# Second head's decay rows in place, clamps on ScalarE, and later loads for heads nine and ten

## Chip, cores and metric

The kernel runs on one core of a Trainium2 chip. The metric is the device time of one execution in microseconds (us). Three runs of the kernel before took 766.26, 769.34 and 770.9 us, so the median is 769.34 us.

## The reference

Three layers follow each other, over 4 batches of 576 positions. B and H below are 4 and 8, so there are 32 attention heads of 64 columns.

```
# attention with a decay
cum    = cumsum(max(s, 0))                       # s: (4, 8, 576)
scores = q k^T / 8 - (cum_i - cum_j), causal     # per head, 576 x 576
attn   = softmax(scores);  x = attn v            # -> (4, 576, 512)
# gated values
gate   = sigmoid(5-tap causal convolution of x with conv_w)
x      = (gate * (x @ w_val)) @ w_out
# mixing of positions (rank 32), then a feed-forward layer of width 2048
u      = x + (x^T U V)^T
out    = u + max(u @ w_ch1, 0) @ w_ch2
```

## The kernel before

**Tiling.** Each head is one step of the loop at L752, `n` from 0 to 32. In step `n` the scores of head `n` are made in five row blocks (`score`, L474) and the probabilities of head `n-1` are transposed (`trans`, L509); after every second head the pair is multiplied with its values (`attn_v`, L533). Once a batch of 8 heads is done, its dense layers are mixed into the steps of the next batch. The feed-forward layer comes last, in TensorE matmuls alone. So the first eight heads run with little beside them but the splitting of the weights (`widen`, L358), which is spread over the steps as side work.

**The decay.** The term cum_j - cum_i enters the score matmul as extra contraction rows under the 64 rows of q and k. Head 0 has two such rows, made in place: VectorE clamps `s` at 0 (L256), scans it (L257) and writes one row under Q and one under K (`row`, L308) from the coefficients in `coef`. The other heads have four rows (KP), taken from E and F: for all 32 heads at once VectorE clamps `sp` (L260), scans it into `cum` (L261), rounds it (L262) and subtracts (L264), and ScalarE multiplies by -8 (L263, L265). Head 1 and head 2 fetch their rows by a transfer from there (L297, `direct`). The rest read them from a copy in device memory (`ef`, L341).

**Two kinds of heads.** Heads 0 to 7, 16 and 30 (`WHOLE`, L85) are loaded straight into their Q and K tiles and multiplied in full fp32. Every other head is loaded as one tile `qk` (`load_raw`, L276, two transfers), split by ScalarE into `hi` and by GpSimd into a rest that lies in Q2 (`prep_head`, L332 and L333), and spread by five transfers into Q1, K1, Q2 and K2 (`high` and `low`, L322 to L330). In the trace these transfers are named K<-hi, Q<-hi and K<-Q. Head 8 is the first such head. Its loads stand in the program at step 6 and head 9's at step 7, but nothing ties them to that step: they need only a free `qk` buffer, of which there are two.

**What sets the order.** All transfers go through SP's queue, in order. A planner lays out the instructions of each engine from a timed model, with a priority by program order and the offset that each kind of work has in `PLAN` (L23); what could run early by the model is moved early. Every engine then works strictly in that order: an instruction that waits holds up all that stands behind it on its engine. `fill` (L468) puts small matmuls without use between the transposes of the first heads, and 13 matmuls of the same sort (`WARM`) stand ahead of the first scores.

Of the kernel before, what the change touches and what calls it, by code (L numbers as in the profile page):

```python
# [11 lines left out]
F32 = mybir.dt.float32  # L12
F32R = mybir.dt.float32r
BF16 = mybir.dt.bfloat16
U32 = mybir.dt.uint32
AF = mybir.ActivationFunctionType
ALU = mybir.AluOpType
# [3 lines left out]


PLAN = {  # L23
    "pace": ("gpsimd", -500),
    "qk_hi": ("scalar", 6000),
    "qk_lo": ("gpsimd", 2000),
    "put": ("sync", 3000),
# [62 lines left out]
ORDER = "T0 T1 S0 T2 T3 S1 S2 S3 T4 S4 A0 A1"  # L90
NPD = 6
DT = {"exp": 0.51, "xh": 0.96, "xl": 0.25, "tap": 1.5, "taps": 0.9, "tanh": 1.83, "gv": 4.3, "nl": 3.6, "rows": 10.0, "prep": 1.51}
WARM = 13


@with_exitstack
def fused_kernel(ctx, tc, qT, kT, vP, s, wval, wout, convw, U, V, w1, w2, rows01, out):
    nc = tc.nc
    B, H, D, S = qT.shape
    P = 128  # L100
# [7 lines left out]
    KP = 4  # L108
# [5 lines left out]
    NH = B * H  # L114
# [20 lines left out]
    def rnd(kind, o, i, by=1.0):  # L135

        eng = Via(kind)
        if eng.name == "scalar":
            eng.mul(o, i, by)  # L139
        elif eng.name == "vector" and by == 1.0:  # L140
            eng.tensor_copy(o, i)
        else:
            eng.tensor_scalar(o, i, by, 0.0, op0=ALU.mult, op1=ALU.add)

    def rest(kind, o, i, hi, by=1.0):

        if by == 1.0:
            Via(kind).tensor_sub(o, i, hi.bitcast(F32))
        else:
            Via(kind).scalar_tensor_tensor(o, i, by, hi.bitcast(F32), op0=ALU.mult, op1=ALU.subtract)  # L150
# [5 lines left out]
    def defer(dt, f, key=None):  # L156
        order[0] += 1
        later.append((clock["now"] + dt, order[0], f, key))
# [56 lines left out]
    at = ctx.enter_context(tc.tile_pool(name="at", bufs=2, side="right"))  # L215
# [15 lines left out]
    def part(b, m, n=S, parts=P):  # L231
        return uT[0:parts, m, b * S:b * S + n]

    sp, cum = (part(1, m, parts=NH) for m in range(2))
    ones, first = part(1, 2), part(1, 3)
    E = [part(2, r, parts=NH) for r in range(KP)]
    F = [part(3, r, parts=NH) for r in range(KP)]
    coef = at1.tile([P, 4], F32, name="coef")
    nc.sync.dma_start(first[64:66, :], s[0, 0:1, :].to_broadcast([2, S]))
    nc.sync.dma_start(coef[64:66, :], rows01)  # L240
    nc.sync.dma_start(sp, s.rearrange("b h s -> (b h) s"))

# [2 lines left out]
    idle = psV.tile([P, 1024], F32, tag="av", name="idle")[:, 0:512]  # L245
    for _ in range(WARM):
        nc.tensor.matmul(idle, warm[:, 0:P], warm, start=True, stop=True)
# [5 lines left out]
    )  # L253
    nc.vector.memset(ones, 1.0)

    nc.vector.tensor_scalar_max(first[64:66, :], first[64:66, :], 0.0)  # L256
    nc.vector.tensor_tensor_scan(first[64:66, :], ones[64:66, :], first[64:66, :], 0.0, op0=ALU.mult, op1=ALU.add)  # L257
    for t, v in ((E[0], 8.0), (E[2], 8.0), (F[1], 1.0), (F[3], 1.0)):
        nc.gpsimd.memset(t, v)
    nc.vector.tensor_scalar_max(sp, sp, 0.0)  # L260
    nc.vector.tensor_tensor_scan(cum, ones[0:NH, :], sp, 0.0, op0=ALU.mult, op1=ALU.add)  # L261
    nc.vector.tensor_copy(F[0].bitcast(F32R), cum)  # L262
    nc.scalar.mul(E[1], F[0], -8.0)  # L263
    nc.vector.tensor_sub(F[2].bitcast(F32R), cum, F[0])  # L264
    nc.scalar.mul(E[3], F[2], -8.0)  # L265
    EF = [uT[0:NH, :, b * S:(b + 1) * S] for b in (2, 3)]


# [3 lines left out]
    hd = {}  # L272

    raw = {}

    def load_raw(n):  # L276

        if n < NH and n not in WHOLE:
            b, h = divmod(n, H)
            raw[n] = at.tile([P, S], F32, tag="qk", name="qk")  # L280
            nc.sync.dma_start(raw[n][0:64, :], qT[b, h])
            nc.sync.dma_start(raw[n][64:, :], kT[b, h])

    def load_head(n, direct=False):
        b, h = divmod(n, H)
        t = hd[n] = {"K": 64 + KP if n else 66, "nm": at.tile([P, 6], F32, tag="nm", name="nm")}
        kind = F32 if n in WHOLE else F32R
        for nm in ("Q1", "K1"):
            t[nm] = at.tile([64 + KP, S], kind, tag=nm, name=nm)
        if n in WHOLE:  # L290
            nc.sync.dma_start(t["Q1"][0:64, :], qT[b, h])
            nc.sync.dma_start(t["K1"][0:64, :], kT[b, h])
        else:
            t["qk"] = raw.pop(n)
        if n:
            for i, nm in enumerate(("Q1", "K1")):
                nc.sync.dma_start(t[nm][64:, :].bitcast(F32), EF[i][n:n + 1] if direct else ef[n, i])  # L297

    def load_values(n):
        b, h = divmod(n, H)  # L300
        hd[n]["V"] = at1.tile([P, 5, 2, D], F32, tag="V", name="V")
        nc.sync.dma_start(hd[n]["V"], vP[b, h // 2])

    def prep_head(n):

        t = hd[n]
        if n == 0:
            def row(o, i):  # L308
                nc.vector.tensor_scalar(
                    o[64:66, :], first[64:66, :], coef[64:66, 2 * i:2 * i + 1], coef[64:66, 2 * i + 1:2 * i + 2],  # L310
                    op0=ALU.mult, op1=ALU.add,
                )
            return [lambda: row(t["Q1"], 0), lambda: row(t["K1"], 1)]
        if n in WHOLE:
            return []
        t["Q2"], t["K2"] = (at.tile([P, S], F32R, tag=nm, name=nm) for nm in ("Q2", "K2"))
        hi, lo = at.tile([P, S], F32R, tag="hi", name="hi"), t["Q2"]

        def put(o, i):
            Via("put").dma_start(o.bitcast(F32), i.bitcast(F32))  # L320

        def high():  # L322
            put(t["Q1"][0:64, :], hi[0:64, :])
            put(t["K1"][0:64, :], hi[64:, :])
            put(t["K2"][0:64, :], hi[64:, :])

        def low():

            put(t["K2"][64:, :], lo[64:, :])
            put(t["Q2"][64:, :], hi[0:64, :])  # L330
        return [
            lambda: rnd("qk_hi", hi, t["qk"]),  # L332
            lambda: rest("qk_lo", lo, t["qk"], hi),  # L333
            high,
            low,
        ]

    load_head(0)
    load_head(1, True)
    for i in range(2):  # L340
        nc.sync.dma_start(ef[:, i], EF[i])  # L341

    for f in prep_head(0):
        f()
    for c in range(5):
        for x in Pt[c]:
            nc.gpsimd.memset(x[:, 0 if c == 0 else CW[c]:], 0.0)
# [33 lines left out]
    def words(ap):  # L381

        return ap.bitcast(U32)
# [40 lines left out]
    pace = []  # L424
# [5 lines left out]
    def load_wide(i):  # L430
        wait_for_pace(ring[i % 3])
        wide[i][0](ring[i % 3])
# [319 lines left out]
    for n in range(NH + 1):  # L752
        phase[0] = n
        if n > 0:
            pace[:] = [hd[n - 1]["nm"][:, 4:5]]
        if 2 <= n + 1 < NH:
            load_head(n + 1, n == 1)
        load_raw(n + 2)
        if n == 1:
            nc.sync.dma_start(craw.bitcast(U32), words(convw))  # L760
        if 1 <= n <= 3:
            load_wide(n - 1)
        if n < NH and n % 2:
            load_values(n)
        m = n - 1
        items = []

        def add(cost, f, *a):
            items.append((cost, f, a))

        ahead, before = n < NH, n > 0
        for x in (ORDER if m % 2 else ORDER0).split():
            kind, i = x[0], int(x[1])
            if kind == "S" and ahead:
                add((0.1, 0.22, 0.32, 0.42, 0.53)[i], score, n, i)
            elif kind == "T" and before:
                add((0.03, 0.21, 0.32, 0.43, 0.55)[i], trans, m, i)
            elif kind == "A" and before and m % 2:
                add((0.96, 1.7)[i], attn_v, m, i)
        if before and m % 2 == 1:  # L780
            add(0.0, norm, m // 2)
        total = sum(x[0] for x in items)
        if before and m % 2 == 1:
            defer(DT["rows"], lambda pr=m // 2: norm_rows(pr))
        if n + 1 < NH:
            for i, f in enumerate(prep_head(n + 1)):
                defer(DT["prep"] * i, f, "prep")
        todo = 0.0
        if dense:
            first, _, done, _ = dense[0]  # L790
            slots = max(1, first + H - n)
            todo = max(0.0, (DENSE - done) / slots)
        clock["dense"] = clock["att"] = 0.0
        for cost, f, a in items:
            f(*a)
            advance(cost)
            clock["att"] += cost
            if n > 0:
                steps[0] += SIDE[(n > 8) + (n > 12) + (n > 17)] * cost / total
                side_step(int(steps[0]))  # L800
                steps[0] -= int(steps[0])
            run_dense(todo * clock["att"] / total)
        if before and m % H == H - 1:
            dense.append([n + 1, dense_work(m // H), 0.0, clock["now"] + DWAIT])
        force("prep")
        if m % 2:
            hd.pop(m, None)
            hd.pop(m - 1, None)
# [192 lines left out]
```

## Time and profile before

| what | value |
|---|---|
| median of 3 runs | 769.34 us (766.26 to 770.9) |
| the profiled execution | 764.93 us, of which the trace spans 762.8 us |
| PE busy | 743.7 us (98%) |
| DVE, ACT, POOL busy | 464.4, 299.2, 291.2 us |
| chain that ended last | PE 85%, DMA 4%, DVE 4%, ACT 3% |
| mean granted TensorE clock | 0.993 |

PE is TensorE, PEld its weight loads, DVE VectorE, ACT ScalarE, POOL GpSimd, and SP (SPq: its sequencer) issues transfers. PE's busy time counts every matmul, the useless ones of the start and of `fill` too, and a matmul that runs at half clock is busy for longer; so 98% is no measure of what PE could still gain in the first microseconds. A row of a timeline or of a list of groups ends with the idle time of its engine just before and with what ended it. In the trace `uT` is also the tile in which `sp`, `cum`, `first`, E and F lie, `P` is a tile of probabilities and `nm` holds the (negated) maxima of a head's rows.

### The profile page before, as it was taken

Reading aid. Unit: us, or ns where it says so; the run is one execution under the profiler, and the core shown is the slowest. Engines: PE = TensorE matmul, PEld = TensorE weight load, DVE = VectorE, ACT = ScalarE, POOL = GpSimd, SP = SyncE. Lnnn points to the kernel's source line nnn. Section 1 sums busy time; section 2 is a strip of 40 time slices with the busy share of each in tenths; the row PEclk is TensorE's granted clock in tenths of the full one; section 3 lists DMA queues with packets and bytes.
Section 4 is the critical chain, followed back from the end, with each engine's and each line's share of the span. In section 5 each row is a group of like instructions: output and inputs, shape, how many; then the busy total and the mean of one; then the engine's idle time right before and its main releaser. Section 6 shows DMA issues by size and latency. Waiting matters only on the chain.

```text
span 762.8 us, 12349 instructions
## 1 busy us (share of the span) xinstructions
PE 743.7 (98%) x4453; PEld 624.8 (82%) x4453; DVE 464.4 (61%) x1052; ACT 299.2 (39%) x785; POOL 291.2 (38%) x321
## 2 busy tenths in 40 slices
PE   8999999899999999999899999999999999999998
PEld 4777888788887998798788888888888888888887
DVE  6798875887657755666749996424582234223234
ACT  4777756875677776633212211111121011001110
POOL 3466754553522233557197765102540024100000
PEclk9999999999999999999999999999999999999999
DMA  5734544644455432021103221100120000000023
GB/s 147 229 120 120 140 118 114 174 119 127 120 124 134 122 100 56 18 85 55 56 1 111 83 87 53 54 1 28 55 85 1 0 28 1 1 0 1 1 111 138
DMA packets 27012, 59.40 MB, mean 78 GB/s; under 512 B 4654, under 2 KB 5294, under 8 KB 26952
## 3 DMA queue, kind: packets, MB, share of 16 engines
q1 hardware_dynamic: 26952, 58.62, 26.9%
q8 instruction: 35, 0.57, 0.3%
q14 instruction: 25, 0.20, 0.1%
HBM read 37.04 MB, written 5.31 MB: 56 GB/s over the span
## 4 chain that ended last, share of the span: by engine, by line
PE 85%; DMA 4%; DVE 4%; ACT 3%; issue 2%; SPq 1%; POOL 0%; ACTq 0%; DVEq 0%
PE d L132 39%; PE acc L132 26%; PE pt L132 8%; PE av L132 6%; PE sc L132 6%; DMA qk<-in_kT 2%; DMA K<-Q 1%; DVE av L604 1%; ACT P L132 1%; DVE P L132 1%; DMA Q<-hi 1%; DVE uT L132 1%; DMA uT<-in_w 0%; ACT PTB L132 0%; ACT hi L132 0%
## 5 line engine op out<-in xcount | busy, mean ns | idle before, releaser
L132 PE MATMUL d<-u,w1h 128*128 128x512 f32 (+1 forms) x640 | 184.2, 371 | 0.0
L132 DVE SCALAR_TENSOR_TENSOR hl<-d,hh 128x512 fp32r<-128x512 f32 (+1 forms) x80 | 50.7, 635 | 170.3 <-ACT hh L861 170.3
L861 ACT ACTIVATE hh<-d 128x512 fp32r<-128x512 f32 (+1 forms) x80 | 44.2, 554 | 274.6 <-PE acc L132 149.5
L132 PEld LDWEIGHTS d<-u,w1h 128*128 128x128 f32 x640 | 116.0, 188 | 22.2
L132 PE MATMUL d<-u,w1l 128*128 128x512 f32 (+1 forms) x320 | 118.6, 371 | 0.0
L132 PE MATMUL acc<-hl,w2h 128*128 128x512 f32 (+1 forms) x320 | 105.0, 371 | 0.0
L132 PE MATMUL acc<-hh,w2h 128*128 128x512 f32 (+1 forms) x320 | 104.4, 372 | 0.5 <-DVE uT L132 0.5
L132 PE MATMUL acc<-hh,w2l 128*128 128x512 f32 (+1 forms) x320 | 102.0, 371 | 0.0
L132 ACT ACTIVATE P<-P,nm 64x64 f32<-64x64 f32 (+4 forms) x160 | 89.0, 560 | 25.2 <-DVE nm L132 24.6
L132 PE MATMUL sc<-K,Q 68*128 68x288 f32 (+11 forms) x384 | 89.1, 344 | 4.6 <-ACT PTB L132 1.8
L132 DVE CUSTOM_DVE_ANT_0 P<-sc,causal 64x64 f32<-64x64 f32 (+4 forms) x160 | 65.2, 421 | 30.8 <-PE sc L132 28.2
L132 PE MATMUL pt<-ident,P 128*128 128x128 f32 x480 | 78.5, 284 | 5.4 <-ACT PTA L139 2.6
L132 DVE TENSOR_TENSOR uT<-acc,uT 128x512 f32<-128x512 f32 (+1 forms) x120 | 70.1, 630 | 22.3 <-PE acc L132 22.2
L132 PEld LDWEIGHTS sc<-K,Q 68*128 68x128 f32 (+2 forms) x384 | 62.2, 193 | 13.2 <-ACT PTB L132 2.6
L132 PEld LDWEIGHTS d<-u,w1l 128*128 128x128 f32 x320 | 60.2, 188 | 11.0
L132 PEld LDWEIGHTS acc<-hh,w2h 128*128 128x128 f32 x320 | 58.7, 188 | 12.1 <-issue 0.9
L132 PEld LDWEIGHTS acc<-hl,w2h 128*128 128x128 f32 x320 | 58.8, 188 | 11.2
L132 PEld LDWEIGHTS acc<-hh,w2l 128*128 128x128 f32 x320 | 58.6, 188 | 11.3
L132 PEld LDWEIGHTS pt<-ident,P 128*128 128x128 f32 x480 | 56.3, 145 | 12.3 <-ACT PTA L139 3.6
L604 DVE SCALAR_TENSOR_TENSOR av<-X,cw,av 128x576 f32<-128x576 f32 x64 | 52.3, 817 | 4.9 <-ACT av L132 4.5
L132 DVE SCALAR_TENSOR_TENSOR scr<-raw,scr 128x512 uint32<-128x512 uint32 (+1 forms) x56 | 52.4, 936 | 1.4
L132 DVE TENSOR_SCALAR scr<-scr 128x512 uint32<-128x512 uint32 x56 | 43.3, 773 | 11.9 <-POOL w1l L132 6.3
(123 smaller groups left out, 1286.9 us busy)
## 6 DMA issues: line engine op xcount, KB each, us to landing
raw<-in_w SPq DMA_DIRECT2D x28, 512.0 KB
K<-hi SPq DMA_DIRECT2D x44, 144.0 KB
Q<-hi SPq DMA_DIRECT2D x44, 144.0 KB
V<-in_vP SPq DMA_DIRECT2D x16, 320.0 KB
out<-uT SPq DMA_DIRECT2D x16, 256.0 KB
qk<-in_qT SPq DMA_DIRECT2D x22, 144.0 KB
qk<-in_kT SPq DMA_DIRECT2D x22, 144.0 KB
K<-Q SPq DMA_DIRECT2D x22, 144.0 KB
```

What stands on the lines that cost most here:

```text
L132: return f(*args, **kw)
L604: Via("tap").scalar_tensor_tensor(g, X[:, k:k + S], cw[:, p, k:k + 1], g, op0=ALU.mult, op1=ALU.add,)
L861: Via("hh").activation(h_, o, AF.Relu)
```

## The change

- Head 1 gets two decay rows made in place, as head 0 has them: a second tile of `s` is loaded ahead of everything but the first, and scan and two rows are run for it on VectorE. It takes no rows from E and F any more.
- The clamps at 0 (two of the small tiles, one of `sp`) move from VectorE to ScalarE as Relu.
- The work on E and F (memsets, scan, rounding, difference, two products) comes after the rows of both heads in the program.
- The loads of heads 8 and 9 are placed in steps 3 and 4, and ahead of each GpSimd copies one column of head 2's or head 3's maxima into the tile to be loaded, so that the transfer can't be issued before that maximum is known. From head 10 on the loads stand where they stood.
- The priority offset of that copy becomes 0, and the matmuls ahead of the first scores become 10.

```diff
-    "pace": ("gpsimd", -500),
+    "pace": ("gpsimd", 0),
...
-WARM = 13
+WARM = 10
...
-    ones, first = part(1, 2), part(1, 3)
+    ones = part(1, 2)
+    first = [part(0, 0), part(0, 1)]
...
-    nc.sync.dma_start(first[64:66, :], s[0, 0:1, :].to_broadcast([2, S]))
+    for i in range(2):
+        nc.sync.dma_start(first[i][64:66, :], s[0, i:i + 1, :].to_broadcast([2, S]))
...
-    nc.vector.tensor_scalar_max(first[64:66, :], first[64:66, :], 0.0)
-    nc.vector.tensor_tensor_scan(first[64:66, :], ones[64:66, :], first[64:66, :], 0.0, op0=ALU.mult, op1=ALU.add)
-    for t, v in ((E[0], 8.0), (E[2], 8.0), (F[1], 1.0), (F[3], 1.0)):
-        nc.gpsimd.memset(t, v)
-    nc.vector.tensor_scalar_max(sp, sp, 0.0)
-    nc.vector.tensor_tensor_scan(cum, ones[0:NH, :], sp, 0.0, op0=ALU.mult, op1=ALU.add)
-    nc.vector.tensor_copy(F[0].bitcast(F32R), cum)
-    nc.scalar.mul(E[1], F[0], -8.0)
-    nc.vector.tensor_sub(F[2].bitcast(F32R), cum, F[0])
-    nc.scalar.mul(E[3], F[2], -8.0)
+    for x in first:
+        nc.scalar.activation(x[64:66, :], x[64:66, :], AF.Relu)
...
+            if H <= n < H + 2:
+                Via("pace").tensor_copy(raw[n][:, 0:1], hd[n - H + 2]["nm"][:, 4:5])
             nc.sync.dma_start(raw[n][0:64, :], qT[b, h])
...
-        t = hd[n] = {"K": 64 + KP if n else 66, ...
+        t = hd[n] = {"K": 64 + KP if n > 1 else 66, ...
...
-        if n:
+        if n > 1:
             for i, nm in enumerate(("Q1", "K1")):
                 nc.sync.dma_start(t[nm][64:, :].bitcast(F32), EF[i][n:n + 1] if direct else ef[n, i])
...
-        if n == 0:
+        if n < 2:
+            x = first[n][64:66, :]
...
-            return [lambda: row(t["Q1"], 0), lambda: row(t["K1"], 1)]
+            return [
+                lambda: nc.vector.tensor_tensor_scan(x, ones[64:66, :], x, 0.0, op0=ALU.mult, op1=ALU.add),
+                lambda: row(t["Q1"], 0), lambda: row(t["K1"], 1),
+            ]
...
-    load_head(0)
-    load_head(1, True)
+    for n in range(2):
+        load_head(n)
+    for n in range(2):
+        for f in prep_head(n):
+            f()
+    for t, v in ((E[0], 8.0), (E[2], 8.0), (F[1], 1.0), (F[3], 1.0)):
+        nc.gpsimd.memset(t, v)
+    nc.scalar.activation(sp, sp, AF.Relu)
+    nc.vector.tensor_tensor_scan(cum, ones[0:NH, :], sp, 0.0, op0=ALU.mult, op1=ALU.add)
+    nc.vector.tensor_copy(F[0].bitcast(F32R), cum)
+    nc.scalar.mul(E[1], F[0], -8.0)
+    nc.vector.tensor_sub(F[2].bitcast(F32R), cum, F[0])
+    nc.scalar.mul(E[3], F[2], -8.0)
     for i in range(2):
         nc.sync.dma_start(ef[:, i], EF[i])
-    for f in prep_head(0):
-        f()
...
-        load_raw(n + 2)
+        if 3 <= n <= 4:
+            load_raw(n + H - 3)
+        elif n + 2 >= H + 2:
+            load_raw(n + 2)
...
-        if n + 1 < NH:
+        if 2 <= n + 1 < NH:
             for i, f in enumerate(prep_head(n + 1)):
```

## Rows read from the trace of the kernel before

**Rows 1.** Busy us (instructions) of each engine by stretch, granted clock, DMA share, GB/s.

```profile
7.00:22.47 15.47, 12.83 (x70) 9.80 (x70) 7.55 (x29) 9.82 (x30) 2.03 (x2) 0.89 0.63 163
22.47:59.47 37.00, 37.00 (x273) 28.35 (x274) 32.52 (x97) 29.18 (x89) 21.83 (x24) 1.00 0.53 160
59.47:110.00 50.53, 47.62 (x371) 40.27 (x370) 41.27 (x116) 34.57 (x98) 32.40 (x34) 1.00 0.50 131
```

**Rows 2.** The chain that ended last, 6 to 23 us: start, length, what.

```profile
6.87 1.36 DVE uT L261
...
8.73 0.76 DVE uT L264
...
10.11 0.67 ACT hi L132
...
12.81 4.17 DMA K<-Q
...
17.54 0.63 SPq L297
...
22.47 0.66 PE pt L132 x4
```

**Rows 3.** Timeline of DVE, 2 to 12 us: start, length, line, operation.

```profile
2.21 1.43 DVE L256 TENSOR_SCALAR uT<-uT 2x576 f32<-2x576 f32 x1
...
5.05 0.70 DVE L260 TENSOR_SCALAR uT<-uT 32x576 f32<-32x576 f32 x1
...
6.28 0.57 DVE L309 TENSOR_SCALAR K<-uT,coef 2x576 f32<-2x576 f32 x1
...
8.25 0.45 DVE L262 CAST uT<-uT 32x576 fp32r<-32x576 f32 x1
...
9.41 0.20 DVE L132 CUSTOM_DVE_ANT_0 P<-sc,causal 64x64 f32<-64x64 f32 x1
...
11.82 0.08 DVE L132 DVE_READ_ACCUMULATOR2_ANT nm<- 128x1 f32 x1
```

**Rows 4.** Timeline of PE, 1 to 13 us.

```profile
1.52 5.03 PE L247 MATMUL idle<-causal 128*128 128x512 bf16 x13 [1.52 <-DVE causal L243]
...
6.90 3.08 PE L132 MATMUL sc<-K,Q 66*128 66x64 f32 x12 [0.34 <-DVE K L309]
...
12.47 0.60 PE L132 MATMUL sc<-K,Q 68*128 68x64 f32 x2 [0.98 <-DVE nm L132]
```

**Rows 5.** Timeline of SP's queue, 10 to 32 us.

```profile
10.37 0.61 SPq L297 DMA_DIRECT2D Q<-uT  x1
...
31.82 0.29 SPq L297 DMA_DIRECT2D K<-ef  x1
```

**Rows 6.** Busy us by stretch of one microsecond, granted clock after the five engines.

```profile
10.00:11.00 1.00, 0.19 (x2) 0.00 (x0) 1.00 (x5) 1.00 (x4) 0.14 (x1) 1.00 0.02 5
...
13.00:14.00 1.00, 1.00 (x7) 0.82 (x6) 0.23 (x2) 0.97 (x5) 0.00 (x0) 0.50 1.04 272
...
15.00:16.00 1.00, 1.00 (x6) 0.77 (x5) 0.37 (x2) 0.14 (x1) 0.00 (x0) 0.52 0.97 244
```

**Rows 7.** Timeline of ACT, 0 to 24 us.

```profile
0.73 1.28 ACT L263 ACT_TABLE_LOAD   x1 [0.73 <-PEq L991]
8.73 0.68 ACT L263 ACTIVATE uT<-uT 32x576 f32<-32x576 f32 x1 [6.72 <-DVE uT L262]
...
21.08 0.68 ACT L132 ACTIVATE hi<-qk 128x576 fp32r<-128x576 f32 x1 [1.72 <-DMA qk<-in_kT]
```

**Rows 8.** Timeline of POOL, 0 to 11 us.

```profile
0.34 0.10 POOL L991 MEMSET const-uint8-127<- 128x1 uint8 x1
...
4.09 1.02 POOL L250 TENSOR_SCALAR_AFFINE_SELECT causal<-causal 128x128 f32<-128x128 f32 x1
...
10.86 1.40 POOL L132 TENSOR_TENSOR Q<-qk,hi 128x576 fp32r<-128x576 f32 x1 [5.41 <-ACT hi L132]
```

**Rows 9.** Timeline of PE, 37 us: the first scores of head 4.

```profile
37.07 0.33 PE L132 MATMUL sc<-K,Q 68*128 68x64 f32 x2
```

More of the change, by code (lines that the diff above doesn't have):

```diff
@@ L285, in load_head @@
         b, h = divmod(n, H)
-        t = hd[n] = {"K": 64 + KP if n else 66, "nm": at.tile([P, 6], F32, tag="nm", name="nm")}
+        t = hd[n] = {"K": 64 + KP if n > 1 else 66, "nm": at.tile([P, 6], F32, tag="nm", name="nm")}
         kind = F32 if n in WHOLE else F32R
@@ L306, in prep_head @@
         t = hd[n]
-        if n == 0:
+        if n < 2:
+            x = first[n][64:66, :]
             def row(o, i):
                 nc.vector.tensor_scalar(
-                    o[64:66, :], first[64:66, :], coef[64:66, 2 * i:2 * i + 1], coef[64:66, 2 * i + 1:2 * i + 2],
+                    o[64:66, :], x, coef[64:66, 2 * i:2 * i + 1], coef[64:66, 2 * i + 1:2 * i + 2],
                     op0=ALU.mult, op1=ALU.add,
                 )
-            return [lambda: row(t["Q1"], 0), lambda: row(t["K1"], 1)]
+            return [
+                lambda: nc.vector.tensor_tensor_scan(x, ones[64:66, :], x, 0.0, op0=ALU.mult, op1=ALU.add),
+                lambda: row(t["Q1"], 0), lambda: row(t["K1"], 1),
+            ]
         if n in WHOLE:
```

## The prediction

> **What bounds the kernel now.** I read the stages first. From 22.47 to 59.47 us PE has no idle microsecond: 37.00 busy of 37.00, at full clock. From 59.47 to 110 it idles 2.9 us, and DVE still has 9.3 us to spare of 50.53 there. Before 22.47 it is another matter: of the 15.47 us from 7.00 on PE is busy for 12.83, at a mean granted clock of 0.89 [rows 1]. So the change, which touches the first heads, is worth what it takes off the time until PE runs dense, and what it puts into the dense stage counts against it.
>
> The chain of waits says what holds the start up, and it isn't PE. It runs over DVE's work on E and F (scan at 6.87, difference at 8.73), then over head 8's split on ACT (10.11), its transfer K<-Q (12.81, 4.17 us long), the issue of head 2's row that stood behind it on SP (17.54), and reaches PE again at 22.47 [rows 2]. The last stretch shows in ACT's rows: the split of head 9 at 21.08 held ACT idle for 1.72 us until its load had landed [rows 7], while an exponential that PE needs stood behind it. Work for heads 8 and 9, six steps ahead of their scores, thus lies in the chain of heads 0 to 2.
>
> Around it: head 0's scores start at 6.90, released by its K row on DVE, and take 3.08 us; head 1's start at 12.47 [rows 4]. PE is said to have waited for a maximum there, but that ended at 11.90 [rows 3]; the later event is head 1's Q row, issued at 10.37 [rows 5], so 2.1 us pass from issue to use. The first maximum comes at 9.41, because scan, rounding and difference of E and F stand ahead of it [rows 3]. From 10 to 11 us PE is busy for 0.19 us, and from 13 to 16 its granted clock is about 0.50, which is the 1.2 GHz level [rows 6].
>
> **The change, part by part.**
>
> *Head 0's rows.* The clamp leaves DVE, where it took 1.43 us from 2.21 on [rows 3], for ACT, where 576 columns take 0.68 us and the one table load ends at 2.01 [rows 7]. The clamp then ends at 2.9, the scan (1.36, as that of `cum` in rows 2) at 4.3 and the two rows (0.57 each [rows 3]) at 5.4, against 6.85 before; that also drops the `sp` clamp (0.70) that stood between them [rows 3]. Not certain: the clamp of 1.43 us lay wholly beside POOL's first memsets, the rows of 0.57 us after the last long instruction of POOL, which ends at 5.1 [rows 3, 8]. The new rows start at 4.3. If both take 1.43, they end at 7.1. So the first score moves by -1.4 to +0.3 us. I take 6.0, a gain of 0.9, since POOL's long work is over at 5.1, in the middle of the first row. One more transfer issue ahead of Q and K (at most 0.61, as the one at 10.37 [rows 5]) fits inside this, since Q and K have until 6.0.
>
> The Trainium skill (SBUF — State Buffer, the section on the two sides of SBUF) says that GpSimd and a VectorE instruction in a two-port mode lock each other out for a whole instruction. By that rule both rows could take the long time, the scores would start at 7.1, and the sum below would be 1.1 us smaller; the row of 1.43 us speaks for it, the end of POOL's work against the second row.
>
> The Trainium skill (ScalarE: Activation LUTs, Rules for kernel authors) puts relu and max on VectorE and not on ScalarE. By it the clamp should lose; the rows say 0.68 on ACT against 0.70 and 1.43 on DVE, so at most nothing is lost, and ACT is idle until 8.73 [rows 7].
>
> *Head 1's rows and the work on E and F.* DVE gains one scan and two rows (1.36 + 1.14 = 2.5 us) and loses the clamps. Head 1's scores no longer wait for E, F and a transfer. E and F are now needed by head 2 alone, whose row was issued at 17.54 [rows 2]; there is cover for them behind head 0's maxima. If that cover is gone, head 2 is late by what they take: 1.36 + 0.45 + 0.76 us on DVE, 0.68 on ACT and 2.1 for the transfer [rows 2, 3, 7].
>
> *How early can PE be dense?* Two floors, both from a first score at 6.0. DVE: 2.5 for head 1's rows, 2.6 for E and F, and twice 2.5 for the maxima of heads 0 and 1 (9.41 to 11.90 [rows 3]) end at 16.1. PE: its 12.83 busy us up to 22.47 hold three at half clock (13 to 16 [rows 6]), an estimated 11.3 us at full clock, which end at 17.3. Before, PE lay 4.1 us above its floor (15.47 - 11.3). Engines that work strictly in order don't reach such a floor: I take half of the 4.1 as gained, between nothing and all. With the start that is 0.9 + 2.1 = 3.0 us, between -0.3 and 5.5.
>
> *What is moved into the dense stage.* Heads 8 and 9 now cost it two splits on ACT (0.68 each), two rests on POOL (1.40 each), two copies on POOL (0.10 each, as its 128x1 memset) and some ten issues on SP with their transfers [rows 7, 8]. Beside 37.00 us of PE there, ACT is busy for 29.18, POOL for 21.83 and the transfer engines for 0.53 [rows 1], so most of it is hidden. Upper bound: both splits hold ACT as at 21.08, 1.72 + 0.68 us each, or 4.8 us; lower bound nothing. I take one split exposed, 0.7 us, nearer the low end since PE's rows there show no idle time at all.
>
> *The new wait.* The copy waits on POOL for the last maximum of head 2 (then 3). Behind it stand POOL's steps of the weight splitting, for which DVE waits; behind the load on SP stand loads of weights, values and the next head. Head 4's last row was issued by 32.11 [rows 5] and used at 37.07 [rows 9]; less 2.1 us for the transfer that is 2.9 us of slack, so a short wait costs nothing.
>
> *The rest.* Three warm-up matmuls fewer end it about 1.2 us earlier (13 took 5.03 [rows 4]), at 5.4, close to the new first score. The priority offset has only the two copies to act on. Neither gets a term of its own.
>
> Sum: 3.0 - 0.7 = 2.3 us gained. The profiled execution took 764.93 us (762.8 of span and 2.1 around it) and lies 4.4 us under the median of the runs; it would become 762.6, and the median of 769.34 becomes **767.0**.
>
> **Rivals.**
> 1. *The gain is absorbed* (0.22). PE's 2.9 idle us from 59.47 to 110 show waits that an earlier start lengthens if their ends hang on DVE's weight splitting. For it: DVE is busy for 32.52 of 37.00 before [rows 1]. Against: that work starts earlier too. Time: 769, within 1.5.
> 2. *POOL and SP stall* (0.12), the case on the slow side. The order is planned from a model; if the maxima come later on the chip than there, POOL stands at the copy and SP behind it. It decides from 2.9 us of stall on. A stall of 5 us at both heads costs 2 x 2.1 us, with the exposed splits 4.8; less the start's 3.0 that is +6.0, or 775. From 771 to 779. Against it: POOL idles 15 of 37 us.
> 3. *A larger gain* (0.12). Both floors are nearly reached (5.5 us) and freer queues shorten later waits, of which 2.9 us lie before 110. All of it would be 8.4 us: 761; from 757 to 763.
> 4. *The change doesn't do what it says* (0.04). The planner puts E and F ahead of head 0's maxima all the same, or gives ACT a second table load (1.28 us [rows 7]) ahead of the exponentials. Time: 768 to 771.
>
> **How the numbers follow.** The forecast has 0.50 and its own range is 763 to 769. The other cases stretch the range: 760.5 takes in most of rival 3, and 774, the bound without any gain at the start and with 4.8 us lost (769.3 + 0.3 + 4.8 = 774.4), half of rival 2. The runs before spread by 4.6 us, or 0.6%, so 1% (7.7 us) is about what a measurement can tell from no change. Faster by over 1% means under 761.6: a good half of rival 3 and some spread of the forecast, 0.13. Slower means over 777.0: a quarter of rival 2 and some mishap of a newly planned order, 0.06. The rest is 0.81.
>
> **What would show it.** In the profile after, the first score of head 0 should come near 6.0 and its first maximum before 8.5; head 1's first score before 11; no split of `qk` before 25 us; the granted clock should stay at its higher level from 13 to 16. PE should run dense from about 19.5 instead of 22.47 and show little idle time until 57. If the start comes 3 us earlier and the end doesn't, rival 1 holds. If SP shows waits of more than 2.9 us at the loads of heads 8 and 9 and PE idles between 30 and 45, rival 2 holds. Wrong altogether would be a start no earlier than before.

## The result: 1% slower

| | before | after |
|---|---|---|
| median | 769.17 us (766.26 to 770.9, 4 runs) | 775.89 us (772.69 to 780.36, 4 runs) |
| ratio, 95% interval | | 1.0101 [1.0062, 1.0141] |
| profiled execution, span | 764.93, 762.8 us | 774.55, 772.8 us |
| mean granted clock of it | 0.993 | 0.986 |

The forecast was 767.0 and its range ended at 774.0. The two profiled executions lie 9.6 us apart and the medians 6.7, since that of before was one of its shortest; so I read places in the traces, and sizes from medians.

**Stages after** (busy us and instructions of PE, PEld, DVE, ACT, POOL, then granted clock, DMA share, GB/s), to be held against [rows 1, 6]:

```profile
7.00:22.47 15.47, 15.39 (x76) 11.41 (x76) 9.14 (x41) 10.36 (x34) 0.42 (x2) 0.78 0.57 177
22.47:59.47 37.00, 34.73 (x254) 26.33 (x252) 30.88 (x88) 27.54 (x84) 22.68 (x25) 1.00 0.55 158
42.00:48.00 6.00, 4.32 (x38) 3.44 (x35) 4.84 (x12) 3.46 (x12) 2.85 (x4) 1.00 0.57 146
78.00:90.00 12.00, 9.75 (x73) 8.31 (x71) 7.07 (x23) 7.45 (x23) 8.02 (x8) 0.86 0.48 120
59.47:110.00 50.53, 45.80 (x353) 38.62 (x353) 39.21 (x110) 32.69 (x95) 30.95 (x31) 0.97 0.48 119
```

Before had from 78 to 90:

```profile
78.00:90.00 12.00, 11.68 (x92) 10.69 (x88) 10.75 (x29) 8.30 (x23) 9.86 (x9) 1.00 0.71 184
```

The stage without an idle microsecond now has 2.27 us of them, 1.68 of these between 42 and 48. From 59.47 to 110 us PE idles 4.7 us instead of 2.9, with a second hole of 2.25 us between 78 and 90, where the granted clock is 0.86 instead of 1.00. In the start PE is busier, but its granted clock is 0.78 instead of 0.89.

**The hole at 45 us.** POOL, then SP, ACT and PE of after (start, length, line, operation, and in brackets the idle time before it and what ended it):

```profile
28.21 0.19 POOL L277 COPY qk<-nm 128x1 f32<-128x1 f32 x1 [1.05 <-DVE nm L132]
...
38.76 1.28 POOL L132 TENSOR_TENSOR wvl<-uT 128x512 fp32r<-128x512 f32 x1 [0.69 <-DVE nm L132]
39.98 0.19 POOL L277 COPY qk<-nm 128x1 f32<-128x1 f32 x1
```

```profile
27.80 0.30 SPq L294 DMA_DIRECT2D K<-ef  x1
28.42 0.47 SPq L278 DMA_DIRECT2D qk<-in_qT  x1
28.94 0.59 SPq L279 DMA_DIRECT2D qk<-in_kT  x1
...
39.05 1.62 SPq L278 DMA_DIRECT2D qk<-in_qT  x2
40.71 1.88 SPq L279 DMA_DIRECT2D qk<-in_kT  x2
```

```profile
31.90 0.69 ACT L132 ACTIVATE hi<-qk 128x576 fp32r<-128x576 f32 x1 [0.31 <-DMA qk<-in_kT]
...
44.83 0.68 ACT L132 ACTIVATE hi<-qk 128x576 fp32r<-128x576 f32 x1 [2.16 <-DMA qk<-in_kT]
45.42 0.76 ACT L132 ACTIVATE P<-P,nm 128x576 f32<-128x576 f32 x1
...
46.18 0.74 ACT L132 ACTIVATE PTB<-pt 128x256 f32<-128x256 f32 x2
...
84.76 0.68 ACT L132 ACTIVATE hi<-qk 128x576 fp32r<-128x576 f32 x1 [4.45 <-DMA uT<-in_U]
```

```profile
35.87 0.43 PE L132 MATMUL sc<-K,Q 68*128 68x64 f32 x2 [0.23 <-DVE nm L132]
...
43.98 0.33 PE L132 MATMUL sc<-K,Q 68*128 68x64 f32 x2
...
46.60 0.55 PE L132 MATMUL av<-PTB,V 128*64 128x192 f32 x4 [1.53 <-ACT PTB L132]
...
54.38 0.33 PE L132 MATMUL sc<-K,Q 68*128 68x64 f32 x2
```

Head 3's last maximum on DVE, the first scores of heads 5 and 6 before, and then the same hole as a chain of waits (start, length, what):

```profile
39.12 0.07 DVE L132 DVE_READ_ACCUMULATOR2_ANT nm<- 128x1 f32 x1
```

```profile
45.14 0.43 PE L132 MATMUL sc<-K,Q 68*128 68x64 f32 x2
...
53.06 0.33 PE L132 MATMUL sc<-K,Q 68*128 68x64 f32 x2
```

```profile
38.77 1.27 POOL wvl L132
40.04 0.14 POOL qk L277
40.19 0.47 SPq L278
...
40.71 4.02 DMA qk<-in_kT
...
44.83 0.16 ACT hi L132
...
45.42 0.85 ACT P L132 x2
46.28 0.28 ACT PTB L132
...
46.60 0.55 PE av L132 x4
```

Head 3's last maximum is known at 39.2 us; the copy for head 9 stands behind a weight step on POOL that ends at 40.04, so the load is issued at 40.2. Its K half is issued next to that of head 10 and lands 4.02 us later. ACT has nothing to do but wait for it: its next instruction is the split of head 9, whose scores come after those of heads 6 to 8, and behind that stand an exponential and the copy PTB that PE wants at once. Heads 4 and 5 start their scores 1.2 us earlier than before (35.87 against 37.07 in [rows 9], 43.98 against 45.14), head 6 starts 1.3 us later (54.38 against 53.06).

The Trainium skill (Perfetto Trace Analysis, the section on the Tensor Engine instruction) says that the queues of ACT, DVE and GPSIMD are strictly first in, first out, while PE's can let weight loads pass. The trace agrees: ACT passes nothing in those 2.16 us.

Ahead of the second hole a split waits again, that of head 12 at 84.76, for 4.45 us. Its load isn't held by any copy. The chain goes back to SP:

```profile
77.37 3.78 DMA K<-Q
81.17 0.46 SPq L132
81.68 0.60 SPq L279
```

Between the two halves of head 12's load SP stands at a transfer Q<-hi until a transfer K<-Q has landed; the K half is issued at 81.68 only. (ACT's row names the load of U, which is issued right behind it.) So ACT stands at a split in both holes, but for two different reasons.

**The start after**, PE and then DVE:

```profile
1.52 3.73 PE L249 MATMUL idle<-causal 128*128 128x512 bf16 x10 [1.52 <-DVE causal L245]
6.59 4.78 PE L132 MATMUL sc<-K,Q 66*128 66x64 f32 x12 [1.34 <-DVE K L308]
...
11.81 0.52 PE L132 MATMUL sc<-K,Q 66*128 66x64 f32 x2
```

```profile
2.93 2.64 DVE L313 TENSOR_TENSOR_SCAN uT<-uT 2x576 f32<-2x576 f32 x2 [0.86 <-ACT uT L259]
5.50 0.55 DVE L308 TENSOR_SCALAR Q<-uT,coef 2x576 f32<-2x576 f32 x1
5.97 0.57 DVE L308 TENSOR_SCALAR K<-uT,coef 2x576 f32<-2x576 f32 x1
...
8.82 0.19 DVE L132 CUSTOM_DVE_ANT_0 P<-sc,causal 64x64 f32<-64x64 f32 x1
```

The scans of both heads run ahead of head 0's rows, so the first score moves from 6.90 to 6.59 only; and it runs at half clock (granted 0.50 from 8 to 14 us), 4.78 us for what took 3.08 [rows 4].

### The profile page after: what moved, and what is told of

The parts are those of the page before. It is cut to its first block, busy times and chain, and to the rows that moved or that the text cites. A ratio compares the mean times of both kernels' runs of the same rounds, so it can differ in the third digit from the quotient of the medians.

```text
span 772.8 us, 12342 instructions
## 1 busy us (share of the span) xinstructions
PE 747.6 (97%) x4450; PEld 627.2 (81%) x4450; DVE 463.9 (60%) x1053; ACT 300.3 (39%) x788; POOL 292.5 (38%) x323
## 4 chain that ended last, share of the span: by engine, by line
PE 80%; DVE 7%; DMA 5%; ACT 4%; issue 1%; SPq 1%; POOL 0%; ACTq 0%; DVEq 0%
PE d L132 37%; PE acc L132 26%; PE pt L132 6%; PE av L132 5%; PE sc L132 5%; DVE uT L132 2%; DVE av L614 2%; DMA qk<-in_kT 2%; DMA uT<-in_w 2%; DVE P L132 1%; ACT P L132 1%; ACT PTA L132 1%; DMA K<-Q 0%; ACT uT L132 0%; ACT nh L139 0%
## 5 line engine op out<-in xcount | busy, mean ns | idle before, releaser
L132 PE MATMUL sc<-K,Q 68*128 68x288 f32 (+13 forms) x384 | 91.9, 352 | 8.2 <-ACT PTB L132 2.9
L132 DVE TENSOR_SCALAR scr<-scr 128x512 uint32<-128x512 uint32 x56 | 43.4, 775 | 11.4 <-POOL w1l L132 6.3
```

Of the source, the lines that this page charges most:

```text
L132: return f(*args, **kw)
```

## Experiments

The theory: the loss is the wait for the maxima, which makes the split of head 9 late on ACT. Rivals: the start itself loses (its scores run at half clock), the moved work costs by its amount, any newly planned order costs as much, or the runs differ by their granted clock. All runs are medians of five rounds against the kernel before; ratios have a 95% interval.

**The start alone**: the kernel after, with heads 8 and 9 loaded as before.

```diff
-            if H <= n < H + 2:
-                Via("pace").tensor_copy(raw[n][:, 0:1], hd[n - H + 2]["nm"][:, 4:5])
...
-        if 3 <= n <= 4:
-            load_raw(n + H - 3)
-        elif n + 2 >= H + 2:
-            load_raw(n + 2)
+        load_raw(n + 2)
```

> Only the start of the change: second head's rows in place, clamps on ScalarE, E and F later, 10 warm-up matmuls; the loads of heads 8 and 9 stand as before, with no copy and no wait. Theory A (the held-back loads and splits of heads 8 and 9 cost the time, in the dense stage): the gain of the start stays, about 1.6 us as in the first product with values (23.7 against 25.3), so 766 to 768.5 against 769.2. Theory B (any new plan of the order lands anywhere within about a per cent, whatever its cause): no sign foreseen, 762 to 778. Theory C (the start itself is worse, by the lower clock): 772 or more.

Measured 770.41 us, 1.0021 [0.9993, 1.0048]. The start doesn't lose what the change loses.

**The wait alone**: the kernel before, with the lines that were taken out above put in, and `pace` at 0.

> Only the held-back loads of heads 8 and 9 with their copies on GpSimd, on the kernel before. Theory A: slower by the whole loss plus the start's gain that is not there, 776 to 780. Theory B: no sign foreseen, 762 to 778. Theory C: no loss, 767 to 771.

Measured 775.94 us, 1.0102 [1.0061, 1.0143]: the whole loss, with the start of before. ACT's row has the same stall:

```profile
48.53 0.68 ACT L132 ACTIVATE hi<-qk 128x576 fp32r<-128x576 f32 x1 [2.89 <-DMA qk<-in_kT]
```

and PE is busy for 3.75 of the 6 us from 48 to 54, at a granted clock of 0.72.

**The warm-up**: the kernel after with `WARM = 13`; and the kernel before with `WARM = 12`, as an edit that should be worth nothing.

> The changed kernel with 13 warm-up matmuls in place of 10. The scores of head 0 took 4.78 us in it and not 3.08, at half clock. Theory A: 1.7 us come back at most, so 774 to 776. Theory B: anything from 762 to 778. Theory C: most of the loss comes back, 768 to 771.

> The kernel before with 12 warm-up matmuls in place of 13, which removes 0.4 us of useless work that ends before the first scores and leaves all else as it was. It measures how far a newly planned order alone moves the time. Theories A and C: within 1.5 us of the kernel before. Theory B: 4 us or more from it, either way.

After with 13: 775.43 us, 1.0082 [1.005, 1.0114]. Its scores of head 0 take 2.98 us instead of 4.78, and the end doesn't notice. Before with 12: 772.37 us, 1.0059 [1.0032, 1.0086]. That was not expected: the planner put many of PE's rows elsewhere, and PE is busy from 59.47 to 110 us for 44.23 us instead of 47.62 [rows 1]:

```profile
59.47:110.00 50.53, 44.23 (x347) 37.88 (x344) 41.08 (x111) 32.32 (x92) 31.10 (x33) 1.00 0.48 125
```

So a new order costs something by itself. The control is `WARM = 14`, where on PE only the added rows differ:

> The kernel before with 14 warm-up matmuls in place of 13: 0.4 us more of useless work, which can delay the first scores by 0.1 us at most. A second measure of what a new plan alone does. Theory A: within 1.5 us of the kernel before. Theory B, with the order before being a good draw that any new plan loses: 2 to 6 us slower, as with 12 of them (3.7 us slower by the median).

Measured 768.13 us, 1.0012 [0.9985, 1.0039]. One matmul costs nothing; the order does.

**The copies without the wait**: the kernel after, copying a constant.

```diff
-                Via("pace").tensor_copy(raw[n][:, 0:1], hd[n - H + 2]["nm"][:, 4:5])
+                Via("pace").tensor_copy(raw[n][:, 0:1], ident[:, 0:1])
```

> The changed kernel with its two copies reading a column of the identity in place of the maxima: the same instructions, but heads 8 and 9 may be loaded from the start as before. It takes away the wait alone. Theory A (the wait puts load and split of heads 8 and 9 where ACT stands still for them): 768 to 771, like the start alone (770.4), and no idle PE from 42 to 48 us. Theory B (a newly planned order costs about half a per cent whatever it is, and the wait adds nothing of its own): 772 to 776, like the changed kernel.

Measured 770.37 us, 1.0036 [1.0012, 1.0061]. Copies and places in the program cost no more than the start alone; both splits go back into the start (10.44 and 12.13 us, without a wait), and PE is busy for all of 42 to 48.

**The same plan without the change**: the planned PE order of the last kernel and of the start alone is, row for row, that of the kernel before with `WARM = 10`.

> The kernel before with 10 warm-up matmuls and nothing else of the change. Its planned order is, on PE, the very order that the start alone and the no-wait copies got (no row differs), and DVE, ACT and SP differ from those by a few rows. So it prices the newly planned order by itself. Theory A (start worth something, plan nothing): 768 to 769.5. Theory B (the new order costs some 2 to 3 us by itself, and the start alone is worth about nothing under one and the same order): 770 to 772.

Measured 771.93 us, 1.0044 [1.0022, 1.0067]. Under one and the same plan the start of the change is thus worth 771.93 - 770.41 = 1.5 us; the intervals overlap, so a gain isn't shown. This kernel loses at the start already: its scores stand behind ten warm-ups as in after, and take 4.99 us.

**Where the loads are held.** Head 10's load held as well (to head 4's maxima, step 5), so that it isn't issued between the halves of head 9's:

> The changed kernel with head 10's load held back as well, to head 4's maxima. In the changed kernel the transfers of heads 9 and 10 were issued in turn and the one that ACT stood waiting for took 4.0 us. Theory A, with the shared transfer as what makes the stall long: ACT's wait for head 9 falls from 2.2 to about 1 us and PE's idle time from 42 to 48 us from 1.7 to below 1; 773 to 775. If the wait itself is the matter: the stall stays, and head 10 adds one, 776 to 779. Theory B: 772 to 776.

Measured 773.01 us, 1.0062 [1.0033, 1.009]: the split of head 9 still waits 1.70 us. Company in the queue is a part of it at most. Both loads two heads earlier (heads 0 and 1, steps 1 and 2):

> The changed kernel with the copies waiting for the maxima of heads 0 and 1 in place of 2 and 3 (steps 1 and 2), so that the loads are issued some 15 us earlier, while PE has less to do. Theory A: most of the stall of 2.2 us on ACT at 44.8 us goes or falls in an earlier stretch, 770 to 774. Theory B: 772 to 776.

Measured 774.02 us, 1.0102 [1.0048, 1.0156], the widest interval of all. The split of head 8 now waits 3.18 us, at 18.79, and PE is busy for all of 22.47 to 59.47, at a granted clock of 0.90; more on this below, under the granted clock. Only head 9 held, and only head 8 held:

> The changed kernel with head 9's load alone held back (to head 3's maxima); head 8 is loaded from the start. Theory A (ACT stands still for head 9's load, 2.2 us, and PE behind it): the loss stays, 773 to 777, with idle PE about 40 to 50 us. Theory B (it is work moved into the dense stage, one split as dear as the other): half the loss comes back, 772 to 774.

> The changed kernel with head 8's load alone held back (to head 2's maxima); head 9 is loaded from the start. In the changed kernel ACT waited 0.31 us for head 8's load. Theory A: the loss goes, 769 to 772, near the no-wait copies (770.4). Theory B: half of it comes back, 772 to 774.

Head 9 alone: 776.42 us, 1.0091 [1.0056, 1.0126], nearly all of the loss. But its head 8 is not loaded from the start, though nothing holds it: the planner puts that load just ahead of head 9's, where it is issued at 38.45 us, and ACT waits for both:

```profile
43.73 0.68 ACT L132 ACTIVATE hi<-qk 128x576 fp32r<-128x576 f32 x1 [1.66 <-DMA qk<-in_kT]
44.76 0.68 ACT L132 ACTIVATE hi<-qk 128x576 fp32r<-128x576 f32 x1 [0.35 <-DMA qk<-in_kT]
```

Head 8 alone: 774.02 us, 1.0067 [1.0034, 1.01], more than I expected. Its head 9 is free, yet the planner puts that load behind head 8's, behind 320 KB of values and 512 KB of weights; the chain shows it landing 5.92 us after its issue, and ACT waits 2.60 us for it:

```profile
31.15 5.92 DMA qk<-in_kT
...
37.08 0.68 ACT hi L132
```

So neither run tells what one head costs without the other.

**Both loads held to head 2's maxima**, in step 3. The same copies, loads and splits are in the dense stage; head 9's load may go 10.7 us sooner (29.48 instead of 40.19), and the planned order changes with it.

```diff
-                Via("pace").tensor_copy(raw[n][:, 0:1], hd[n - H + 2]["nm"][:, 4:5])
+                Via("pace").tensor_copy(raw[n][:, 0:1], hd[2]["nm"][:, 4:5])
...
-        if 3 <= n <= 4:
-            load_raw(n + H - 3)
+        if n == 3:
+            load_raw(H)
+            load_raw(H + 1)
```

> The changed kernel with both loads held back to head 2's maxima, at step 3. The same work lies in the dense stage, but head 9's load is issued some 10 us earlier and needn't share the queue with head 10's. Theory A: no stall of 2 us at head 9's split, 769.5 to 772. Theory B (moved work costs by itself): 773 to 777.

Measured 766.53 us, 0.9981 [0.9954, 1.0009]: the loss is gone. SP, ACT and the stages of this kernel:

```profile
28.79 0.59 SPq L279 DMA_DIRECT2D qk<-in_kT  x1
29.48 0.54 SPq L278 DMA_DIRECT2D qk<-in_qT  x1
30.06 0.59 SPq L279 DMA_DIRECT2D qk<-in_kT  x1
```

```profile
31.78 0.68 ACT L132 ACTIVATE hi<-qk 128x576 fp32r<-128x576 f32 x1 [0.22 <-DMA qk<-in_kT]
...
33.92 0.69 ACT L132 ACTIVATE hi<-qk 128x576 fp32r<-128x576 f32 x1
```

```profile
22.47:59.47 37.00, 36.53 (x273) 27.93 (x271) 31.87 (x90) 28.96 (x84) 25.08 (x27) 1.00 0.58 163
42.00:48.00 6.00, 6.00 (x55) 4.84 (x54) 4.71 (x13) 3.61 (x11) 2.80 (x4) 1.00 0.89 238
78.00:90.00 12.00, 11.06 (x91) 10.65 (x87) 10.51 (x25) 7.38 (x19) 8.77 (x9) 1.00 0.73 179
```

Head 9 follows head 8 at once, its split finds the data there, and both holes of after close or shrink. The start of the first product with the values of each pair (the rows `av<-PTA,V`) shows where after falls behind this kernel:

| us | pair 0 | 1 | 2 | 3 | 4 | 8 | 15 |
|---|---|---|---|---|---|---|---|
| before | 25.33 | 40.38 | 56.39 | 74.54 | 91.05 | 177.85 | 317.38 |
| after | 23.73 | 39.79 | 59.42 | 77.81 | 97.18 | 188.05 | 327.42 |
| both held to head 2 | 23.58 | 39.67 | 57.29 | 72.76 | 90.95 | 177.94 | 315.99 |
| after less the last | 0.2 | 0.1 | 2.1 | 5.0 | 6.2 | 10.1 | 11.4 |

Level up to pair 1; then 2.0 us are lost over the stall, 2.9 from pair 2 to 3, where DVE's work is ordered otherwise (from 66 to 78 us DVE is busy for 12.00 us in after and for 9.59 here), 1.2 over the second hole, 3.9 more by pair 8, where part is a granted clock of 0.92 from 160 to 190 us against 1.00, and 1.3 behind it. The medians of the two differ by 9.4 us, and the profiled execution of the last kernel is its shortest (763.22). So the stall at head 9's split accounts for about 2 us by itself. That the rest follows from it is argued: the kernels differ in their planned order too, and an order alone cost up to 0.6%.

**The granted clock.** The executions also differ in their mean granted clock. The four of after ran at 0.984 to 0.989; of before's 115 executions beside the experiments the lowest ran at 0.984 and the middle one at 0.991. So part of the difference of the medians comes with a lower clock, and I compare at the same clock. After's four lie 2.8 to 8.3 us above before's medians there (of 1 to 27 executions each), the wait alone 4.7 to 7.8 us above where before has any, and both loads held to head 2's maxima within 2.6 us of them. The wait's cost is there at an equal clock too. With both loads two heads earlier it is otherwise: at 0.987 and 0.989 that kernel took 771.50 and 768.08 us, where before has medians of 770.60 and 769.74, and three of its six executions ran at 0.976 to 0.982, below any of before, and took 776.55 to 779.47. So its 1.0102 is no evidence of what its wait costs. Whether the holes of a kernel lower its clock is open.

**More from the start?** The last kernel with `WARM = 13`; with the second tile of `s` loaded and clamped only after head 0's Q and K; and with both:

> Both loads held to head 2's maxima, with 13 warm-up matmuls in place of 10; the planned order differs from that kernel's in 16 of 4264 rows on PE. It asks what the missing three cost. If the half clock of head 0's scores matters (3.9 to 5.9 us for the 12 matmuls in place of 3.1): 1 to 2 us faster than with 10, 764 to 766, and the scores take 3.1 us. If the time is lost again behind it: within 0.7 us of 766.5.

> Both loads held to head 2's maxima, and the second head's s is loaded and clamped behind head 0's Q and K, so that its scan no longer stands ahead of head 0's rows; the order on PE is the same. It asks whether that scan is why the first scores came at 6.6 and not at 6.0 or before. If so: first scores at 5.3 to 5.8, and 0.5 to 1.2 us less time, 765 to 766.5. If Q and K land no earlier than 6.4, nothing moves.

> Both of these: second s later and 13 warm-up matmuls, which end at about 6.9. First scores then follow the warm-up at about 6.9, at full clock. 764 to 766.5; if the earlier rows and the full clock each counted by themselves, it is no better than the kernel with 13 alone, since the warm-up then sets the first scores.

They took 766.09, 768.15 and 767.01 us, ratios 0.9982 [0.9948, 1.0015], 1.0015 [0.9985, 1.0045] and 1.0001 [0.997, 1.0031]. The second puts the first score at 5.60 us, and pair 0 starts at 23.58 as without it: its first maximum comes at 9.49, behind the scan of head 1 and the work on E and F. None beats the kernel before measurably.

## Why the prediction was wrong

**The new wait**, costed at nothing ("so a short wait costs nothing"), is the step that failed: alone it measured 1.0102 [1.0061, 1.0143]. The prediction asked what stands behind the copy on POOL and behind the load on SP, and found 2.9 us of slack for head 4's rows. That part held: they are out at 27.80, ahead of the held loads, and head 4 starts earlier than before. It did not ask who stands in order in front of the held data. That is ACT, and the very row was quoted, the split of head 9 with its 1.72 us [rows 7]; but that row went into an upper bound only, and not into the price of the wait. The wait moved this row out of the start, where other stalls run beside it, into a stage in which PE has nothing to spare, and made it 2.16 us.

**What is moved into the dense stage**, 0.7 us between bounds of 0 and 4.8, was mis-sized by its reason: "nearer the low end since PE's rows there show no idle time". A stage without idle time has no cover against a late instruction. As amounts, the moved splits, rests and copies cost nothing that can be measured: with both loads held to head 2's maxima they are all there, and the time is 0.9981 of before. With the wait for head 3's maxima they cost 1.0102 alone and 1.0101 with the start, about 7 us where the upper bound had 4.8.

**Everything after** was taken to stay in place. It didn't: the planner gave another order, with a second wait of 4.45 us on ACT at 84.76, and an order changed by one dummy matmul cost 0.59%. The prediction had that as "some mishap of a newly planned order" and gave it no term. The wait alone has the second wait too (4.64 us); head 9 held alone has only 1.81 us there and still nearly the whole loss, so that wait isn't needed for it. What exactly costs the plans with 12 and 10 warm-ups their 0.4 to 0.6% is open. The first shows a split waiting for 1.69 us at 82.89, but with both loads held to head 2's maxima one waits for 1.75 us at 84.64, and that kernel isn't slower.

**The start**, 3.0 us forecast, brought 1.6 at pair 0. The clamps on ACT cost what was said (two in 1.25 us from 2.22), the rows took 0.55 and 0.57 us, no split of `qk` stood before 31.90, and PE is busy for all of 10 to 11 us. But the scan of head 1 was planned ahead of head 0's rows (first score 6.59, not 6.0), the first maximum came at 8.82 and not before 8.5, head 1's first score at 11.81 and not before 11, and the granted clock was 0.50 from 8 to 14 us and 0.69 from 14 to 15, where the higher level was expected from 13 to 16. The warm-ups, without a term, cost 1.7 us on head 0's scores; with 13 pair 0 starts at 22.58. As a time, the start was worth 1.5 us under one plan, by medians whose intervals overlap.

The Trainium skill's rule on the port that GpSimd and VectorE share (SBUF — State Buffer, the section on its two sides) was not put to the test at the rows of after: POOL's last memset ended at 4.70 us, before the first row began at 5.50. With the second `s` later the first row began at 4.37, beside POOL's last memsets (until 4.75), and took 0.69 us; that is far from the 1.43 that the prediction allowed for. In the dense stage of after there is a case that looks like the rule: between 22 and 60 us one and the same DVE instruction (a TENSOR_SCALAR of 128x512) took 0.41 to 0.50 us seven times and 1.52 us at 45.85, beside POOL's rest of head 9 (45.60 to 47.09). So a moved rest can cost DVE about 1 us, which the prediction had not priced; no run isolates it.

**The rivals.** The second has the right time (775, for 775.89), but by luck: PE's hole (45.1 to 46.6) lies just behind the place that it named (30 to 45), and its mechanism isn't what happened. SP's queue was not held up for head 4, and its point of 2.9 us decided nothing; a wait of 2.16 us on ACT opened the hole. The first, an absorbed gain, describes the start alone (1.0021). The chance of 0.06 for slower by over 1% was too low, as I see it, because waits were priced where the queue was short of time, and not where the data were wanted next.

## What to carry to other kernels

A transfer that is held back must be released a whole landing time (here 4 to 6 us with other loads beside it) before the planned place of the first instruction that reads it, on an engine that works in order; who waits behind that instruction pays, however late the data are really needed. Where a planner writes the order, an edit that does nothing tells what a new order alone costs: here up to 0.6%, twice the gain that was forecast. Hold both sides to medians: one profiled execution stood over 4 us under its median. Compare the granted clocks as well, when the difference is 1% or less.

## What the runs showed of the hardware

- The same transfer of 144 KB landed 4.02 us after its issue with a second load issued beside it, and 5.92 us after it behind 320 and 512 KB.
- Twelve scores of head 0 take 2.97 to 3.08 us at the upper clock level and 4.78 to 4.99 at the lower or mostly lower one. After 1.34 us of idle PE the clock fell (after), after 1.30 it didn't (before with 12 warm-ups, 3.08 us), and the start alone and its twin with copies took 3.08 and 5.92 us for them, though the granted clock reads 1.00 over the scores of both. I draw no rule from that.
- Executions of one kernel differ with the mean granted clock: the start alone took 766.07 us at 1.000 and 773.85 at 0.982, as much as the whole effect of the change.
